# A fused attention and mixture-of-experts kernel: output scatters that do not wait for each other, early loads of the dense stage's first block, and a last block summed part by part

## Chip, cores and metric

One core of a Trainium2 chip runs the whole program. The metric is the time of one execution on the device, in microseconds (us); lower is better.

## What is computed

Three stages follow each other, all in float32 (B 4, H 8, S 576, D 64 in the attention; 2304 tokens of width 512 after it):

```python
q_rot, k_rot = rotate(q), rotate(k)                       # rotary embedding
attn = softmax(q_rot @ k_rot.T / sqrt(D)); x = attn @ v   # -> 2304 x 512
e = argmax(x @ w_gate); gate = softmax(x @ w_gate)[e]     # 8 experts, one per token
x = gate * (relu(x @ w1[e]) @ w2[e])                      # 512 -> 1024 -> 512
h = x @ moe2_w_in                                         # dense: 512 -> 2048 -> 512
out = (relu(h) ** 2) @ moe2_w_out
```

## The kernel before, in words

**Products.** TensorE multiplies in pairs: each operand is split into a high part (rounded by ScalarE) and a low part (what is left, subtracted on VectorE or GpSimd), and a product is three matmuls, high by high, high by low, low by high.

**Stages.** Attention takes 16 pairs of heads. The expert stage takes the tokens sorted by expert, in tiles of 128 rows: `Experts.run` (L916 to L922) loops over tiles `i` 2 to 17, and the last tiles sit in nested conditionals (`tail`, L941). The dense stage, `Dense.run` (L1096 to L1117), takes 6 blocks `b` of 384 rows; for each block 16 steps `f` compute 128 columns of h and add their share of the output.

**One step of the expert loop.** `begin(i)` is the first product of tile i into PSUM `p_h` (`first`, L861), the gather of tile i+2 (L843, an indirect transfer on POOL's queue), the transposes of tile i+1 (`turn_x`, L850), and `change(i+1, 0)` (L902): only if the expert changes, the first weight matrix W1 is split from its raw buffers (high parts on ScalarE L838, low parts L839, the second of the four chunks on POOL), and then the next expert's raw weights are loaded by SP (L817), each chunk once its buffer has been read. `second(i-1)` is the second product of the tile before (L890): VectorE scales it into `yo` (L894), and POOL scatters it to the DRAM buffer `yd` (L895). `end(i)` transposes tile i's relu (`turn_h`, L880) and does `change(i, 1)`, the same for W2 (loads L819). Then `extra(i - 2)` slips in work for the dense stage: its weights' loads and conversions (L962, L973 to L984) and, at the end of steps 14 to 16, `load_part` (L1037): one third of the dense stage's first block of 384 rows, read from `yd` by SP into `row`; one buffer holds all three in turn. At the end of steps 15 to 17, `turn_x(0, c)` (L1051 to L1053) transposes such a third into PSUM `p_r` and splits it. A third is thus loaded at the end of one step and transposed at the end of the next.

**Dependencies.** A tile framework places the waits, in the order in which the code names the instructions; it takes an indirect scatter to touch all of its target. Thus a `load_part` waits for the last scatter into `yd` named ahead of it, and the next scatter waits until that load has been read. Each engine and each DMA queue runs its own instructions in that same order, so one that waits holds up all behind it on its queue. SP issues all the plain loads here.

**The dense stage's end.** Two steps after `first(b, f)` (L1061), `second(b, f)` (L1074) adds the step's share to three PSUM tiles `o[c]`, one per 128 rows, three matmuls each (L1082). After step 15, `store` (L1085) copies them to SBUF `os` (ScalarE for c = 0 and 2, VectorE for c = 1) and POOL scatters each to `out` by the token ids in `id` (L1093):

```python
for f in range(16):          # lagging by two steps
    for c in range(3):       # o[c] += gs[f][c] @ Wo[f], three matmuls
```

Of the kernel before, what the change touches and what calls it, by code (L numbers as in the profile page):

```python
# [12 lines left out]
I32 = mybir.dt.int32  # L13
U32 = mybir.dt.uint32
AF = mybir.ActivationFunctionType
# [7 lines left out]
N, DM = B * S, H * D  # L23
# [3 lines left out]
NA = 2  # L27
# [32 lines left out]
def shape_constants():  # L60
# [27 lines left out]
    for b in range(B):  # L88
        for c in range(4):
# [22 lines left out]
           out=[33.418, 34.148, 36.917, 39.025, 37.411, 29.788, 32.958, 38.405, 36.294, 35.538, 34.643],  # L112
# [623 lines left out]
class Experts:  # L736
# [176 lines left out]
            self.load(m, e)  # L913
            self.split(m, ())

    def run(self, extra):  # L916
        for i in range(NA, 18):
            self.begin(i)
            self.second(i - 1)
            self.end(i)  # L920
            extra(i - NA)
        self.tail(18)  # L922
# [64 lines left out]
class Dense:  # L987


    def __init__(self, nc, ident, big, wip, words, wp, ps, y, out, w_in, w_out):  # L990
        self.nc, self.ident, self.big, self.words, self.wp, self.ps = nc, ident, big, words, wp, ps
        self.y, self.out, self.w_in, self.w_out = y, out, w_in, w_out
        self.wip = wip
        self.T = {}

    def load_in(self, j):
        self.T["wi", j] = self.words.load(self.w_in[:, 512 * j:512 * j + 512].rearrange("(k p) f -> p k f", p=128), 4)
# [73 lines left out]
        nc.scalar.activation(gs[:, 0], g, AF.Copy)  # L1071
        nc.vector.tensor_sub(gs[:, 1], g, gs[:, 0].bitcast(F32))  # L1072

    def second(self, b, f):  # L1074
        nc = self.nc
        if f == 0:
            self.T["o", b] = [self.ps.tile([128, 512], F32, name="o", tag=f"o{c}", bufs=1) for c in range(3)]
        gs, W = self.T["gs", b, f], self.T["Wo", f]
        for c in range(3):
            n = 0  # L1080
            for a, w in ((0, 0), (0, 1), (1, 0)):
                nc.tensor.matmul(self.T["o", b][c], gs[:, a, 128 * c:128 * c + 128], W[:, w], start=(f == 0 and n == 0), stop=(f == 15 and n == 2))  # L1082
                n += 1

    def store(self, b):  # L1085
        nc = self.nc
        for c in range(3):
            t = self.wp.tile([128, 512], F32, name="os", tag="os", bufs=3)
            if c == 1:
                nc.vector.tensor_copy(t, self.T["o", b][c])  # L1090
            else:
                nc.scalar.activation(t, self.T["o", b][c], AF.Copy)  # L1092
            nc.gpsimd.indirect_dma_start(out=self.out, out_offset=bass.IndirectOffsetOnAxis(ap=self.T["id", b][:, c:c + 1].bitcast(U32), axis=0),  # L1093
                                         in_=t, in_offset=None)

    def run(self):  # L1096
        nb, lag = N // 384, 2
        self.split_in(1)
        for i in range(16 * nb + lag):
            b, f = divmod(i, 16)  # L1100
            if b < nb:
                self.first(b, f)
                if i == 0:
                    self.split_out(0)
                if b == 0:
                    self.weights(f)
                if f == 2:
                    self.load_ids(b)
                    if b + 1 < nb:
                        self.load_x(b + 1)  # L1110
                if f in (10, 12, 14) and b + 1 < nb:
                    self.turn_x(b + 1, f // 2 - 5)
            if i >= lag:
                b2, f2 = divmod(i - lag, 16)
                self.second(b2, f2)
                if f2 == 15:
                    self.store(b2)  # L1117

    def weights(self, f):

# [14 lines left out]
def body(tc, a, cols):  # L1135
    nc = tc.nc
    stack = contextlib.ExitStack()
    with stack:
        pool = lambda name, bufs, **kw: stack.enter_context(tc.tile_pool(name=name, bufs=bufs, **kw))
        pp, dp = pool("p", 1), pool("d", 1, space=DRAM)  # L1140
        xd = dp.tile([N, DM], F32, name="xd")
        yd = dp.tile([N + 128, DM + 16], F32, name="yd")
        ident = pp.tile([128, 128], F32, name="ident")
        make_identity(nc, ident)
        tpool = lambda name, **kw: tc.tile_pool(name=name, bufs=1, reuse_waits="tile", **kw)
        rowp = contextlib.ExitStack()
        keep = stack.enter_context(tc.tile_pool(name="keep", bufs=1, side="right"))
        rows = rowp.enter_context(tc.tile_pool(name="row", bufs=1, side="right"))
        consts = rows.tile([128, a["consts"].shape[1]], F32, name="consts")
        cst = lambda n: consts[:, cols[n][0]:cols[n][1]]  # L1150
        R = Route(nc, pp, rows, keep, cst, ident)
        X = Experts(tc, R, rowp.enter_context(tc.tile_pool(name="raws", bufs=1, side="right")), ident, xd, yd, a["moe_w1"], a["moe_w2"])
        w1p = contextlib.ExitStack()
        with tc.manual_schedule():
            done, last = attention(tc, a["rope"], ident, a["qk"], a["v"], a["moe_w_gate"], xd, R.batch,
                                   lambda: nc.sync.dma_start(out=consts, in_=a["consts"]),
                                   lambda at, psum: X.ahead(at, psum, lambda n: w1p.enter_context(tpool(n, side="right"))))
            done.close()
            big, cvp, x0 = [stack.enter_context(tpool(n)) for n in ("big", "cv", "x0")]
            words = Words(nc, cvp)  # L1160
            dn = Dense(nc, ident, big, None, words, None, None, yd, a["out"], a["moe2_w_in"], a["moe2_w_out"])
            with w1p, tpool("xg") as xg, tpool("mw") as mw, tpool("mps", space=PSUM) as ps:
                X.late(big, xg, ps, mw)
                dn.xs0 = x0.tile([128, 2, 4, 384], F32R, name="xs0")
                spots = iter([X.p_r[:, 0:40].rearrange("p (c e) -> p c e", e=8), X.p_r[:, 64:72]])
                R.psum = lambda shape: next(spots)
                X.first(0, 0)
                X.first(0, 1)
                X.swap(0)
                X.relu(0)  # L1170
                next(last)
                next(last, None)
                R.places(dn.xs0)
                for n, eng in enumerate((nc.gpsimd, nc.vector)):
                    R.gated_rows(R.al[n], 10 * n, 10, eng)
                X.first(1)
                X.turn_h(0)
                X.relu(1)
                R.lists(X.p_r[:, 128:128 + 3 * NB].rearrange("p (i t) -> p i t", i=3))
                tokens = R.tokens()  # L1180
                next(tokens)
                X.gather(2)
                X.gather(3)
                R.control()
                next(tokens, None)
                X.second(0)
                X.turn_x(2)
                X.load(0, X.num(1, 0, mx=7, engines=(E.SP,)))
                X.change(2, 0)
                X.turn_h(1)  # L1190
                X.swap(1)
                X.load(1, X.num(1, 0, mx=7, engines=(E.SP,)))

                dn.y0 = R.row.rearrange("p c n -> p (c n)")[:, 2048:2560].bitcast(F32)
                dn.wi0 = R.row.rearrange("p c n -> p (c n)")[:, 0:2048].rearrange("p (a k f) -> p a k f", a=2, k=4)

                def extra(i):
                    if 13 <= i < 16:
                        dn.turn_x(0, i - 13, X.p_r.rearrange("p (k n) -> p k n", k=4))
                    if 12 <= i < 15:  # L1200
                        dn.load_part(i - 12)
                    if i == 14:
                        dn.split_in(0)
                    if i < 9:
                        if i < 8:
                            dn.load_in(i)
                        if i > 0:
                            dn.convert_in(i - 1)
                    if 10 <= i < 14:
                        dn.load_out(i - 10)  # L1210
                    if i in (11, 12):
                        dn.convert_out(i - 11)

                X.run(extra)
            rowp.close()
            with tpool("Wi", side="right") as wi, tpool("dw") as dw, tpool("dps", space=PSUM) as ps:
                dn.wip, dn.wp, dn.ps = wi, dw, ps
                dn.run()
# [25 lines left out]
```

## Time and profile before

| what | value |
|---|---|
| median of 3 runs (lowest to highest) | 992.5 us (991.63 to 993.58) |
| the profiled execution: its own time, and the span of its instructions | 993.26 us, 991.2 us |
| mean granted TensorE clock | 0.993 of full speed |
| TensorE matmuls busy | 955.0 us, 96% |
| VectorE, ScalarE, GpSimd busy | 534.3, 421.7, 320.3 us |
| stages by the timeline of TensorE | attention and routing, then expert tiles up to 573 us, then the dense blocks |

The span runs from the first instruction to the last; 2.06 us of the execution's own time lie around it. The share of busy time is a mean over stages with different limits, so what a change is worth has to be read from the stretch that it touches: who waits there, and what the wait is for.

### The profile page before, as it was taken

To read this page: it belongs to the slowest core of one execution; us is meant where nothing else is said; L and a number is where in the kernel's file an instruction comes from. 1 tells how busy PE (TensorE), PEld (TensorE's weight loads), DVE (VectorE), ACT (ScalarE), POOL (GpSimd) and SP (SyncE) were. 2 spreads that over 40 slices of the span, in tenths; PEclk is the share of its full clock that TensorE was granted. 3 is DMA by queue.
4 is the path that set the end of the run, shared out by engine and by line. 5 is a ranking of instruction groups with operands and counts; after the bars stand their busy time and mean duration, and the time that the engine had idled before them with its cause. 6 is when DMAs were issued, how large, how long until landed. Compare 5 with 4: busy or idle time off the path is not lost. (4 is left out here: it accounts for less than half of the span.)

```text
span 991.2 us, 15383 instructions
## 1 busy us (share of the span) xinstructions
PE 955.0 (96%) x5519; PEld 819.2 (83%) x5519; DVE 534.3 (54%) x935; ACT 421.7 (43%) x834; POOL 320.3 (32%) x241
## 2 busy tenths in 40 slices
PE   4999999999999999999979999999999999999995
PEld 4787878787778888888868789999999999999994
DVE  5677777777868255682884479423322223222221
ACT  3666666675542233442653367422322322222221
POOL 4786888796384111331453300010000100100101
PEclk9999999999999999999999999999999999999998
DMA  6776767775542733363575423100100100000000
GB/s 232 240 199 193 231 203 195 237 199 140 181 138 104 276 129 129 108 234 130 187 272 172 160 91 125 33 32 1 43 22 1 64 1 33 32 1 1 32 1 32
DMA packets 45135, 119.81 MB, mean 121 GB/s; under 512 B 8176, under 2 KB 8176, under 8 KB 42608
## 3 DMA queue, kind: packets, MB, share of 16 engines
q1 hardware_dynamic: 39808, 101.58, 32.8%
q0 software_dynamic: 4960, 16.43, 4.7%
q8 instruction: 45, 0.74, 0.3%
q10 hardware_dynamic: 272, 0.66, 0.2%
q14 instruction: 50, 0.41, 0.1%
HBM read 79.93 MB, written 15.11 MB: 96 GB/s over the span
## 5 line engine op out<-in xcount | busy, mean ns | idle before, releaser
L1082 PE MATMUL o<-Wo,gs 128*128 128x512 f32 x864 | 214.5, 393 | 0.0
L1061 PE MATMUL h<-xs,Wi 128*128 128x384 f32 x1008 | 189.6, 336 | 0.0
L1061 PEld LDWEIGHTS h<-xs,Wi 128*128 128x128 f32 x1008 | 178.1, 188 | 6.6
L1082 PEld LDWEIGHTS o<-Wo,gs 128*128 128x128 f32 x864 | 160.0, 188 | 28.3
L1070 DVE SCALAR_TENSOR_TENSOR g<-h,r 128x384 f32<-128x384 f32 x80 | 44.6, 558 | 190.7 <-ACT r L1066 190.7
L1093 POOL DMA_INDIRECT out_dram<-os,id x18 | 19.1, 1064 | 393.2 <-ACT os L1092 362.1
L293 ACT ACTIVATE e<-ps,mx 128x576 f32<-128x576 f32 x144 | 106.2, 740 | 84.8 <-DVE mx L286 84.7
L286 DVE TENSOR_REDUCE mx<-ps 128x1 f32<-128x576 f32 x144 | 105.9, 753 | 58.0 <-PE ps L278 50.5
L1066 ACT ACTIVATE r<-h 128x384 f32<-128x384 f32 x96 | 47.1, 491 | 204.6 <-PE h L1061 204.6
L890 PE MATMUL p_y<-W,hh 128*128 128x512 f32 x504 | 122.9, 399 | 0.8 <-ACTq L902 0.8
L861 PE MATMUL p_h<-W,xs 128*128 128x512 f32 x480 | 115.8, 397 | 0.0
L890 PEld LDWEIGHTS p_y<-W,hh 128*128 128x128 f32 x504 | 93.1, 188 | 22.2 <-ACTq L902 1.1
L861 PEld LDWEIGHTS p_h<-W,xs 128*128 128x128 f32 x480 | 89.2, 190 | 18.7 <-DVEq L902 0.7
L311 PE MATMUL pp<-ident,e 128*128 128x128 f32 x640 | 85.5, 273 | 2.1 <-DVE eT L327 1.9
L1072 DVE TENSOR_TENSOR gs<-g,gs 128x384 fp32r<-128x384 f32 x96 | 53.5, 558 | 55.9 <-ACT gs L1071 55.3
L433 POOL TENSOR_TENSOR qk<-qk,TB 128x1280 f32<-128x1280 f32 x28 | 81.4, 2924 | 0.0
L311 PEld LDWEIGHTS pp<-ident,e 128*128 128x128 f32 x640 | 74.4, 141 | 3.3 <-DVE eT L327 2.3
L276 PE MATMUL ps<-kZ,qZ 128*128 128x288 f32 x300 | 71.5, 328 | 0.5 <-ACT e L293 0.2
L1071 ACT ACTIVATE gs<-g 128x384 fp32r<-128x384 f32 x96 | 50.4, 525 | 50.4 <-DVE g L1070 49.9
L338 PE MATMUL av<-eT,V 128*64 128x288 f32 x512 | 69.1, 412 | 0.0
L327 DVE COPY eT<-pp 128x512 f32<-128x512 f32 x96 | 64.3, 684 | 4.6 <-PE pp L311 2.7
L895 POOL DMA_INDIRECT yd<-yo,idx x21 | 22.2, 1059 | 134.7 <-DVE yo L894 94.1
(236 smaller groups left out, 1210.4 us busy)
## 6 DMA issues: line engine op xcount, KB each, us to landing
qk<-in_qk_dram SPq DMA_DIRECT2D x15, 1280.0 KB, 6.4
raw<-in_moe_w_dram SPq DMA_DIRECT2D x30, 512.0 KB, 4.8
kZ<-XH SPq DMA_DIRECT2D x60, 160.0 KB, 2.8
rawa<-in_moe_w_dram SPq DMA_DIRECT2D x18, 512.0 KB, 3.5
w<-in_moe_w_in_dram SPq DMA_DIRECT2D x8, 1024.0 KB, 5.2
w<-in_moe_w_out_dram SPq DMA_DIRECT2D x8, 1024.0 KB, 4.9
V<-in_v_dram SPq DMA_DIRECT2D x16, 320.0 KB, 2.9
qZ<-XH SPq DMA_DIRECT2D x30, 160.0 KB, 2.9
```

What stands on the lines that cost most here:

```text
L276: nc.tensor.matmul(t[:, u, 0:288], Q1[:, qs], K1[:, k0 + 288 * u:k0 + 288 * u + 288], start=i == 0, stop=False)
L286: nc.vector.tensor_reduce(small("mx", P, 9)[:, s:s + 1], T["S", P, s][:, :, 0:288], axis=AX.XY, op=ALU.max, negate=True)
L293: nc.scalar.activation(ed.rearrange("p (u n) -> p u n", u=2), T["S", P, s][:, :, 0:288], AF.Exp, bias=T["mx", P][:, s:s + 1], accum_out=SS ...
L311: nc.tensor.transpose(t[:, c * 128:c * 128 + 128], src, ident)
L327: nc.vector.tensor_copy(o, i)
L338: nc.tensor.matmul(t[64 * j:64 * j + 64], V[:, j, kc], eT[:, j, kc, cs] if kc < 4 else eL[:, cs], start=kc == 0, stop=kc == 4)
L433: v.tensor_tensor(out=out, in0=a, in1=b, op=ALU.mult)
L861: nc.tensor.matmul(t[u], s[:, a, k], W1[:, b, k, 512 * u:512 * u + 512], start=n == 0, stop=n == 11)
L890: nc.tensor.matmul(t, s[:, a, k], W2[:, b, k], start=n == 0, stop=n == 23)
L1061: nc.tensor.matmul(t, W[:, a, k, fs], s[:, c, k], start=n == 0, stop=n == 11)
L1072: nc.vector.tensor_sub(gs[:, 1], g, gs[:, 0].bitcast(F32))
L1082: nc.tensor.matmul(self.T["o", b][c], gs[:, a, 128 * c:128 * c + 128], W[:, w], start=(f == 0 and n == 0), stop=(f == 15 and n == 2))
```

## The change

Three edits. `between(i - 2)`, a new hook, stands inside the step, behind `second(i-1)` and ahead of `end(i)`; the transposes and the loads of the dense block's thirds go from `extra` to it. `apart` declares the output scatters to be free of each other, and each scatter reads its ids from a small tile `at` that POOL copies first. For the last block the last two steps are done tile by tile: all that is left of `o[0]`, then its store, then `o[1]`, then `o[2]`; and each of these three stores is copied half by VectorE and half by ScalarE.

```diff
     def run(self, extra, between):
         for i in range(NA, 18):
             self.begin(i)
             self.second(i - 1)
+            between(i - NA)
             self.end(i)
             extra(i - NA)
...
+    def apart(self, ins):
+
+        self.tc.declare_no_dep(ins, group="out", reason="every token's row is written once")
+        self.tc.add_to_no_dep_group("out", ins)
...
+    def store(self, b, cs=range(3)):
...
-            if c == 1:
-                nc.vector.tensor_copy(t, self.T["o", b][c])
+            o = self.T["o", b][c]
+            if b == N // 384 - 1:
+                nc.vector.tensor_copy(t[:, 0:256], o[:, 0:256])
+                nc.scalar.activation(t[:, 256:512], o[:, 256:512], AF.Copy)
+            elif c == 1:
+                nc.vector.tensor_copy(t, o)
...
+            at = self.wp.tile([128, 1], I32, name="at", tag="at", bufs=3)
+            nc.gpsimd.tensor_copy(at, self.T["id", b][:, c:c + 1])
+            put = nc.gpsimd.indirect_dma_start(out=self.out, out_offset=bass.IndirectOffsetOnAxis(ap=at.bitcast(U32), axis=0),
+                                               in_=t, in_offset=None)
+            self.apart(put.ins)
...
-                self.second(b2, f2)
-                if f2 == 15:
-                    self.store(b2)
+                if b2 < nb - 1 or f2 < 16 - lag:
+                    self.second(b2, f2)
+                    if f2 == 15:
+                        self.store(b2)
+        for c in range(3):
+            for f in range(16 - lag, 16):
+                self.second(nb - 1, f, [c])
+            self.store(nb - 1, [c])
...
+                def between(i):
                     if 13 <= i < 16:
                         dn.turn_x(0, i - 13, X.p_r.rearrange("p (k n) -> p k n", k=4))
                     if 12 <= i < 15:
                         dn.load_part(i - 12)
+
+                def extra(i):
                     if i == 14:
                         dn.split_in(0)
```

SP's loads in step 15, before, from the last load of W1's raw weights on (`raw_3727`; `raw_3728` to `raw_3731` are W2's four raw chunks, `row<-yd` is the second third):

```order
L817 DMA raw_3727<-in_moe_w_dram 128x1024
...
L819 DMA raw_3728<-in_moe_w_dram 128x2x512
L819 ISA
L819 DMA raw_3729<-in_moe_w_dram 128x2x512
L819 ISA
L819 DMA raw_3730<-in_moe_w_dram 128x2x512
L819 ISA
L819 DMA raw_3731<-in_moe_w_dram 128x2x512
L902 UNCONDITIONAL_BRANCH x2
L1037 DMA row<-yd 128x512
L962 DMA w_6196<-in_moe_w_out_dram 128x2x1024
```

And now:

```order
L817 DMA raw_3727<-in_moe_w_dram 128x1024
L902 UNCONDITIONAL_BRANCH x2
L1043 DMA row<-yd 128x512
...
L819 DMA raw_3728<-in_moe_w_dram 128x2x512
L819 ISA
L819 DMA raw_3729<-in_moe_w_dram 128x2x512
L819 ISA
L819 DMA raw_3730<-in_moe_w_dram 128x2x512
L819 ISA
L819 DMA raw_3731<-in_moe_w_dram 128x2x512
L902 UNCONDITIONAL_BRANCH x2
L963 DMA w_6196<-in_moe_w_out_dram 128x2x1024
```

The load of the third has gone ahead of the four weight loads; steps 14 and 16 change alike. On TensorE, each of the three groups of four transposes `p_r` moves from behind the eight transposes `p_t` to ahead of them.

At the program's end, with what each instruction waits for (SW and HW are DMA queues' semaphores), ScalarE and POOL before, the last block's stores:

```order
L1092 ACTIVATE os<-o 128x512 [waits DMASW5_49,PE_49]
L1092 ACTIVATE os<-o 128x512 [waits DMASW7_49,PE_49]
...
L1093 DMA out_dram<-os,id 2304x512 [waits DMAHW0_49,DMASW7_49,Activation_49]
L1093 DMA out_dram<-os,id 2304x512 [waits DMASW0_49,DVE_49]
L1093 DMA out_dram<-os,id 2304x512 [waits DMASW1_49,Activation_49]
```

And now, the last two of the three (the first is alike):

```order
L1099 ACTIVATE os<-o 128x256 [waits DMASW3_49,DMASW6_49,DMASW0_49,DVE_49]
L1099 ACTIVATE os<-o 128x256 [waits DMASW7_49,DVE_49]
...
L1105 COPY at<-id 128x1 [waits DMASW6_49]
L1106 DMA out_dram<-os,at 2304x512 [waits Activation_49,Pool_49]
L1105 COPY at<-id 128x1 [waits DMASW7_49]
L1106 DMA out_dram<-os,at 2304x512 [waits Activation_49,Pool_49]
```

A scatter no longer waits for the DMA semaphore of the scatter ahead of it (the SW ones that are left on the copies are those of the block before, whose buffers they take over); POOL's copy of the ids stands between the scatters; and ScalarE's half of a store waits for VectorE, no longer for TensorE.

## Rows read from the trace of the kernel before

**Rows 1.** The page, section 1: busy time, share of the span, instructions.

```profile
PE 955.0 (96%) x5519; PEld 819.2 (83%) x5519; DVE 534.3 (54%) x935; ACT 421.7 (43%) x834; POOL 320.3 (32%) x241
```

**Rows 2.** Waits of TensorE, 455 to 577 us: who for whom, us, times, longest.

```profile
PE p_r L1051 <- DMA row<-yd: 5.6, 1, 5.6
```

**Rows 3.** Timeline of TensorE: start, us, line, out<-in, count, idle before it.

```profile
488.86 5.85 PE L890 MATMUL p_y<-W,hh 128*128 128x512 f32 x24
...
501.69 5.85 PE L890 MATMUL p_y<-W,hh 128*128 128x512 f32 x24
...
507.38 1.03 PE L880 MATMUL p_t<-ident,hs 128*128 128x128 f32 x8
513.98 1.09 PE L1051 MATMUL p_r<-ident,row 128*128 128x128 f32 x4 [5.56 <-DMA row<-yd]
514.72 6.67 PE L861 MATMUL p_h<-W,xs 128*128 128x512 f32 x24
...
521.57 5.84 PE L890 MATMUL p_y<-W,hh 128*128 128x512 f32 x24
...
528.48 5.72 PE L861 MATMUL p_h<-W,xs 128*128 128x512 f32 x24
```

**Rows 4.** Windows: us, busy us (instructions) by engine, TensorE clock, DMA share, GB/s.

```profile
514.00:516.00 2.00, 2.00 (x7) 1.81 (x8) 1.58 (x3) 1.42 (x3) 1.35 (x1) 0.50 0.48 146
```

**Rows 5.** Timeline of SP's queue in steps 15 and 16.

```profile
501.21 4.84 SPq L819 DMA_DIRECT2D raw<-in_moe_w_dram  x4
506.42 0.34 SPq L1037 DMA_DIRECT2D row<-yd  x1
```

**Rows 6.** By tile or line: issue to landing of `row`, W2 raw weights, `yd` scatters.

```profile
DMA to landing us min/median/max: 2.6/6.1/7.4
...
DMA to landing us min/median/max: 4.4/5.9/7.4
...
DMA to landing us min/median/max: 2.8/2.9/7.3
```

**Rows 7.** Timelines of VectorE, GpSimd and ScalarE in steps 15 and 16.

```profile
498.12 0.74 DVE L894 TENSOR_SCALAR yo<-p_y,sg 128x512 f32<-128x512 f32 x1
...
499.64 1.01 POOL L895 DMA_INDIRECT yd<-yo,idx  x1 [2.53 <-issue]
...
514.65 2.00 POOL L895 DMA_INDIRECT yd<-yo,idx  x1 [8.94 <-DVE W L839]
...
513.46 1.06 ACT L838 ACTIVATE W<-raw 128x1024 fp32r<-128x1024 f32 x1 [0.58 <-SPq L902]
```

**Rows 8.** Timeline of the end of the span, all engines.

```profile
978.36 0.60 ACT L1092 ACTIVATE os<-o 128x512 f32<-128x512 f32 x1 [3.11 <-PE o L1082]
...
979.23 0.97 POOL L1093 DMA_INDIRECT out_dram<-os,id  x1 [52.80 <-ACT os L1092]
979.74 0.60 ACT L1092 ACTIVATE os<-o 128x512 f32<-128x512 f32 x1 [0.78 <-PE o L1082]
982.75 0.97 POOL L1093 DMA_INDIRECT out_dram<-os,id  x1 [2.54 <-DMA out_dram<-os,id]
986.58 0.97 POOL L1093 DMA_INDIRECT out_dram<-os,id  x1 [2.86 <-issue]
```

**Rows 9.** Landing of the output scatters; two gathers in a row; a small copy.

```profile
DMA to landing us min/median/max: 2.7/2.7/3.1
...
272.29 1.21 POOL L843 DMA_INDIRECT xg<-xd,idx  x1 [6.80 <-DVE sg L656]
273.80 0.96 POOL L843 DMA_INDIRECT xg<-xd,idx  x1 [0.30 <-issue]
...
569.48 0.20 POOL L893 COPY yo<-idx 128x16 int32<-128x16 int32 x1 [1.84 <-DMA yd<-yo,idx]
```

**Rows 10.** Groups by form: line, engine, op, shapes, count | us, mean ns.

```profile
L367 DVE TENSOR_TENSOR xr<-pj,rs 128x256 f32<-128x256 f32 x16 | 6.6, 415 | 0.0
...
L341 ACT ACTIVATE X<-av 128x288 f32<-128x288 f32 x32 | 12.8, 409 | 7.4 <-PE av L338 7.4
```

More of the change, by code (lines that the diff above doesn't have):

```diff
@@ L914, in swap, with run @@
             self.split(m, ())
-    def run(self, extra):
+    def run(self, extra, between):
         for i in range(NA, 18):
@@ L987, with __init__ @@
 class Dense:
-    def __init__(self, nc, ident, big, wip, words, wp, ps, y, out, w_in, w_out):
-        self.nc, self.ident, self.big, self.words, self.wp, self.ps = nc, ident, big, words, wp, ps
+    def __init__(self, tc, ident, big, wip, words, wp, ps, y, out, w_in, w_out):
+        self.tc, self.nc, self.ident, self.big, self.words, self.wp, self.ps = tc, tc.nc, ident, big, words, wp, ps
         self.y, self.out, self.w_in, self.w_out = y, out, w_in, w_out
@@ L1072, in first, with second @@
         nc.vector.tensor_sub(gs[:, 1], g, gs[:, 0].bitcast(F32))
-    def second(self, b, f):
+    def second(self, b, f, cs=range(3)):
         nc = self.nc
@@ L1078, in second @@
         gs, W = self.T["gs", b, f], self.T["Wo", f]
-        for c in range(3):
+        for c in cs:
             n = 0
@@ L1083, in second @@
                 n += 1
-    def store(self, b):
+    def store(self, b, cs=range(3)):
         nc = self.nc
-        for c in range(3):
+        for c in cs:
             t = self.wp.tile([128, 512], F32, name="os", tag="os", bufs=3)
-            if c == 1:
-                nc.vector.tensor_copy(t, self.T["o", b][c])
-            else:
-                nc.scalar.activation(t, self.T["o", b][c], AF.Copy)
-            nc.gpsimd.indirect_dma_start(out=self.out, out_offset=bass.IndirectOffsetOnAxis(ap=self.T["id", b][:, c:c + 1].bitcast(U32), axis=0),
-                                         in_=t, in_offset=None)
+            o = self.T["o", b][c]
[4 more added lines that the diff above has]
+                nc.vector.tensor_copy(t, o)
+            else:
+                nc.scalar.activation(t, o, AF.Copy)
+            at = self.wp.tile([128, 1], I32, name="at", tag="at", bufs=3)
[3 more added lines that the diff above has]
+            self.apart(put.ins)
     def run(self):
@@ L1160, in body @@
             words = Words(nc, cvp)
-            dn = Dense(nc, ident, big, None, words, None, None, yd, a["out"], a["moe2_w_in"], a["moe2_w_out"])
+            dn = Dense(tc, ident, big, None, words, None, None, yd, a["out"], a["moe2_w_in"], a["moe2_w_out"])
             with w1p, tpool("xg") as xg, tpool("mw") as mw, tpool("mps", space=PSUM) as ps:
@@ L1195, in body @@
                 dn.wi0 = R.row.rearrange("p c n -> p (c n)")[:, 0:2048].rearrange("p (a k f) -> p a k f", a=2, k=4)
-                def extra(i):
+                def between(i):
                     if 13 <= i < 16:
@@ L1212, in extra @@
                         dn.convert_out(i - 11)
-                X.run(extra)
+                X.run(extra, between)
             rowp.close()
```

## The prediction

> **What bounds the kernel now.** I read the page first: TensorE is busy for 96% of the span [rows 1]. So time can be won where TensorE idles or runs slowly, and where the program goes on after its last matmul, and lost by new idle time on it. The waits of TensorE in the late expert tiles then name one long one: 5.6 us, once, for the transfer into `row` [rows 2]. TensorE's timeline shows its place: the transposes `p_r` of the second third, at 513.98 us [rows 3].
>
> What the wait costs is more than its length, and the same rows give it. From one `second` to the next is 501.69 - 488.86 = 12.83 us in step 15, whose transposes waited for nothing. In step 16 it is 521.57 - 501.69 = 19.88 us. The excess is 7.05 us: 5.56 of idle time, and the rest from slow matmuls behind it. The first product took 6.67 us where it takes 5.72 [rows 3], at a granted clock of 0.50 [rows 4], the lower of the two levels (1.2 of 2.4 GHz), after the idle time.
>
> Why was the third late? Its load stands on SP's queue behind four loads of W2's raw weights; these go out from 501.21 us on, as their buffers come free, and the third's goes out at 506.42 [rows 5]. It takes the full 7.4 us to land, as long as the slowest weight load in front of it [rows 6]. A second victim is POOL's scatter into `yd`, which had to wait until 514.65 [rows 7] for that load to be done with `yd`.
>
> Last, the end. The last matmul ends near 979.7 us, when the third copy starts; then three scatters follow each other 3.5 and 3.8 us apart, at 979.23, 982.75 and 986.58 [rows 8], each waiting for the one before, which takes 2.7 us to land [rows 9]. From the start of the last one to the end of the span are 991.2 - 986.58 = 4.62 us, which stay: landing, and the program's closing.
>
> **The change, part one: the thirds.** Nothing is added; three loads and three sets of transposes move.
>
> The second third's load now stands ahead of the four weight loads. What it waits for next is the scatter of the tile before, named just ahead of it: that goes out at 499.64 us and takes a median 2.9 us to land [rows 6, 7], so the load goes out at 502.55, 3.9 us earlier than before. With no weight load in front of it I take the shortest landing of such a load, 2.6 us [rows 6]: 505.2 us. TensorE wants it behind `second`, at 507.38 [rows 3]. The wait goes, with 2.2 us to spare: 7.05 us.
>
> The first third waited for nothing before; its load now goes out behind a scatter too, a few us ahead of its transposes. The third third goes out only after SP has passed the next conditional, which is held until the last W2 load has landed (before, that was near 513.4 us, just ahead of ScalarE's split at 513.46 [rows 7]). Say 515; with the median 6.1 us [rows 6] it lands at 521, while TensorE would be at it one step later than 507.38, at 507.38 + 12.83 = 520.2. With 2.6 us it lands at 517.6. The bounds are thus 0 and about 0.9 us; I take 0, since only the 1 MB load of dense weights may lie in front of it.
>
> What is late next: W2's weights. They are queued behind a load that waits. The first of them goes out at 503.0, not 501.21; the other three are held by their buffers until about 503.5 to 505.8, as before. In front of them are 0.25 MB more. The 2 MB took from 501.21 to 513.46, so an eighth more is 1.5 us, and the last lands near 515 us rather than 513.4. Its high part needs 1.06 us on ScalarE [rows 7]: ready at 516.1. TensorE, no longer held, starts that `second` at 501.69 + 12.83 = 514.52 and reads the last chunk of W2 at its seventh matmul, 6 x 0.24 us later (24 take 5.84 [rows 3]), at 515.96. I book 0.3 us of new waiting (bounds 0 and 1.1, if the loads slip by 0.8 more). ScalarE and VectorE take the third's split 0.6 to 0.7 us earlier in the step, ahead of the relu's split; VectorE's loss falls within the time in which its second subtraction of W2 was blocked, so the buffers come free as before. If that cover is missing, it is in the 1.1 us. POOL's scatter moves from 514.65 to about 509.1; it is off the path.
>
> Part one: 7.05 - 0.3 = **6.75 us**, between 5.0 and 7.05.
>
> **Part two: the end.** TensorE does the same matmuls, so it ends as before. But the first sum is done after 15 of the last 27 matmuls, not after 21. Two sums are 979.74 - 978.36 = 1.38 us apart [rows 8], six matmuls, so the first is ready at 978.36 - 1.38 = 976.98, the second at 978.36, the third, as ever, at 979.74.
>
> Each copy is cut in two, but the order of the instructions shows ScalarE's half waiting for VectorE's, so they add up. VectorE's nearest row of that size is 0.415 us (reading PSUM), ScalarE's 0.409 for 288 columns [rows 10]; I take 0.39 for 256 and 0.03 between. That is 0.84 us, against 0.60 for a whole copy [rows 8]: the cut costs 0.24 us. Were the halves to run side by side it would gain 0.18 us. No row has two engines reading one PSUM tile. The Trainium skill, PSUM — Partial Sum Buffer, section "PSUM bank collisions raise a hardware error", says that two engines must not touch the same bank and partitions at once, reads included; by that rule the halves can only add up, and no run here shows it.
>
> From VectorE's `yo` to its scatter POOL took 499.64 - 498.86 = 0.78 us [rows 7]; ScalarE's copy to the scatter of [rows 8] took 0.27, with nothing but that wait left. Now a semaphore instruction stands in front again, so I take 0.78. The first scatter starts at 976.98 + 0.84 + 0.78 = 978.60 and holds POOL for 0.97. Then come the small copy of ids, 0.20, and a scatter that waits for nothing more, 0.30 behind it as between two gathers [rows 9]: 1.47 us from scatter to scatter. The second starts at 980.07, the third at 981.54; its own copy would allow 979.74 + 0.84 + 0.78 = 981.36. Two transfers in flight are nothing new: two gathers went out 1.5 us apart [rows 9], less than any landing of an indirect transfer in these rows. The end is then 981.54 + 4.62 = 986.16: **5.04 us** saved.
>
> Bounds: POOL free and a lag of 0.27 give 980.85 + 4.62, 5.7 us (6.2 if the halves also overlap). The longest lag is that of the last scatter, 986.58 - (982.75 + 2.73) = 1.1 us; paid three times, the third starts at 983.4: 3.2 us.
>
> The 15 earlier scatters and their copies of ids lie beside TensorE's work, which nothing there waits for; without that cover each copy would be 0.20 us.
>
> **Sum.** 6.75 + 5.04 = 11.8 us off the profiled execution's 993.26: 981.5 us. That execution lies 0.8 above the median of 992.5, so I forecast **980.7 us**.
>
> **Rivals.**
> - *The third is still late.* If the load at 502.55 takes 7.4 us all the same, because weights issued behind it share the engines, it lands at 509.95: TensorE waits 2.6 us, with a like share of slow matmuls (1.49 x 2.57 / 5.56 = 0.7). Part one shrinks to 3.8 us: 983.7 us. For it: landings vary from 2.6 to 7.4. Against: the 7.4 had loads in front. 12%.
> - *The scatters stay slow*, with the long lag each: 3.2 us in place of 5.0, 982.5 us. For it: the lag did vary from 0.27 to 1.1. 14%.
> - *The scatters are not free of each other after all*, or share something that the order doesn't show: the first starts at 978.60 rather than 979.23, and the rest follow as before; 0.6 us saved, 985.1 us. Against: the DMA semaphores are gone from the waits. 2%.
> - *Slower: weights in place of the third.* SP stands before the third's load until the scatter lands, and W2's weights stand behind it. The longest such landing was 7.3 us [rows 6]: load at 506.9, weights from 507.3, the last some 12 us later at 519.6, its high part at 520.7, so TensorE waits 4.7 us, and part one is down to about 1. To eat part two and 2 us more, the weights have to be 14 us late, landing after 529 us: 995 us. That is the point from which it decides; that 7.3 itself waited among weight loads. 2%.
> - *The halves run side by side* or POOL is quicker: 979.6 us. 3%.
>
> **How the numbers follow.** The forecast's own case has the remaining 67%, from 979.4 (7.05 and 5.7 us) to 982.3. Range: low is the best of both, 7.05 and 6.2 us, less the 0.9 us by which the fastest run shown lies under the median: 978.4. High takes in the late third and the slow scatters each by itself: 984.0; both together and the rest are left out. A measurement of this kernel tells about 0.2%, 2 us, from no change; all but the last rival's 2% and a remainder of 1% lie beyond that on the fast side.
>
> **What would show it.** In the waits of TensorE no wait for `row`, and the spacing of `second` near 12.8 us in step 16, with at most a fraction of a us for the split of W2; SP's third ahead of the four weight loads at about 502.5. At the end, three scatters about 1.5 us apart, the first near 978.6 less what was won before, ScalarE's halves starting when VectorE's end, 4.6 us from the last scatter's start to the end. Wrong would be a new wait of TensorE for W2 of over 1.1 us, a landing of the second third of over 5 us, or scatters still 3.5 us apart.

## The result, and the profile after

The changed kernel takes 981.35 us (median of 4 runs, 980.48 to 983.31), the kernel before beside it 992.41 us (4 runs): a ratio of 0.989, 95% interval 0.9871 to 0.9909. The forecast was 980.7 us. Measured once more, with other runs of the kernel before (992.39), it took 981.36 us, ratio 0.9886 (0.987 to 0.9901). The profiled execution took 982.04 us with a span of 980.2 us, 11.0 us less than the 991.2 us of the one before. One execution of e2 below took 1365.34 us at a mean granted clock of 0.656 and stays out of its numbers.

The page after, section 1, answers to [rows 1]: TensorE is busy 1.2 us less, and its mean granted clock is 0.997, against 0.993.

```profile
PE 953.8 (97%) x5519; PEld 818.1 (83%) x5519; DVE 531.9 (54%) x937; ACT 421.5 (43%) x835; POOL 322.5 (33%) x259
```

Waits of TensorE after, 455 to 577 us (who for whom, us, times, longest), to be held against [rows 2]:

```profile
PE p_r L1057 <- DMA row<-yd: 1.2, 1, 1.2
...
PE p_y L890 <- ACT W L838: 0.6, 1, 0.6
```

The wait for `row` is down from 5.6 to 1.2 us, not to nothing, and one for W2's split has come. Their place, in TensorE's timeline after (start, us, line, out<-in, count, idle before), beside [rows 3]:

```profile
487.62 5.85 PE L890 MATMUL p_y<-W,hh 128*128 128x512 f32 x24
...
500.45 5.85 PE L890 MATMUL p_y<-W,hh 128*128 128x512 f32 x24
507.47 0.66 PE L1057 MATMUL p_r<-ident,row 128*128 128x128 f32 x4 [1.16 <-DMA row<-yd]
...
514.69 1.65 PE L890 MATMUL p_y<-W,hh 128*128 128x512 f32 x6
516.92 4.47 PE L890 MATMUL p_y<-W,hh 128*128 128x512 f32 x18 [0.58 <-ACT W L838]
...
522.46 5.74 PE L861 MATMUL p_h<-W,xs 128*128 128x512 f32 x24
```

I measure part one from the first row to the last: 522.46 - 487.62 = 34.84 us, against 528.48 - 488.86 = 39.62 us in [rows 3]: **4.78 us** won, where 6.75 were forecast. It splits by step. Step 15 to 16 takes 514.69 - 500.45 = 14.24 us, 1.41 over the 12.83 of a step without a wait; from that `second` to the next first product are 7.77 us, where 6.92 are needed without a wait (experiment e10 below), 0.85 over. And 7.05 - 1.41 - 0.85 = 4.79.

SP's queue after (start, us, line) shows why; it answers to [rows 5]:

```profile
503.68 0.33 SPq L1043 DMA_DIRECT2D row<-yd  x1
505.51 2.33 SPq L819 DMA_DIRECT2D raw<-in_moe_w_dram  x4
```

The third does go out ahead of the four weight loads, but at 503.68, 5.3 us after the scatter at 498.39 for which it waits, and the weights another 1.83 us later.

The end after, all engines, beside [rows 8]:

```profile
971.04 0.42 DVE L1098 COPY os<-o 128x256 f32<-128x256 f32 x1 [1.15 <-PE o L1088]
971.50 0.38 ACT L1099 ACTIVATE os<-o 128x256 f32<-128x256 f32 x1 [2.20 <-DVE os L1098]
...
972.66 0.98 POOL L1106 DMA_INDIRECT out_dram<-os,at  x1 [55.88 <-ACT os L1099]
...
973.65 0.19 POOL L1105 COPY at<-id 128x1 int32<-128x1 int32 x1
973.79 0.42 DVE L1098 COPY os<-o 128x256 f32<-128x256 f32 x1 [0.95 <-PE o L1088]
974.12 0.98 POOL L1106 DMA_INDIRECT out_dram<-os,at  x1 [0.28 <-POOL at L1105]
...
975.58 0.99 POOL L1106 DMA_INDIRECT out_dram<-os,at  x1 [0.28 <-POOL at L1105]
```

Three scatters 1.46 us apart. From the start of the third sum's copy to the end are 980.2 - 973.79 = 6.41 us, against 991.2 - 979.74 = 11.46 us before: **5.05 us** won, 5.04 forecast. The rest of the 11.0 us, 1.2, was there before the moved instructions began: the `second` of step 14 starts at 487.62 against 488.86. Of that, 1.1 us arose near 267 us, where TensorE waited twice in the execution before, 0.23 us and then:

```profile
267.57 1.22 PE L311 MATMUL pp<-ident,e 128*128 128x128 f32 x8 [0.85 <-DVE eT L327]
```

### The profile page after: what moved, and what is told of

It reads as the page before. It is cut to its first block, busy times and chain, and to the rows that moved or that the text cites. A ratio compares the mean times of both kernels' runs of the same rounds, so it can differ in the third digit from the quotient of the medians.

```text
span 980.2 us, 15407 instructions
## 1 busy us (share of the span) xinstructions
PE 953.8 (97%) x5519; PEld 818.1 (83%) x5519; DVE 531.9 (54%) x937; ACT 421.5 (43%) x835; POOL 322.5 (33%) x259
## 5 line engine op out<-in xcount | busy, mean ns | idle before, releaser
L1106 POOL DMA_INDIRECT out_dram<-os,at x18 | 17.8, 986 | 369.5 <-DVE os L1101 309.9
L895 POOL DMA_INDIRECT yd<-yo,idx x21 | 21.2, 1012 | 124.8 <-DVE yo L894 90.4
```

## Experiments

In the list below "stretch" is the time from the `second` of step 14 to the first product of step 17 (39.62 us before, 34.84 after), and "end" that from the start of the third sum's copy to the end of the span (11.46 and 6.41).

**The parts alone.** e1 is the change without its end:

```diff
-                if b2 < nb - 1 or f2 < 16 - lag:
-                    self.second(b2, f2)
...
-            if b == N // 384 - 1:
-                nc.vector.tensor_copy(t[:, 0:256], o[:, 0:256])
...
-            self.apart(put.ins)
```

> Only the first part of the change: loads and transposes of the thirds in the middle of the step, the end as it was. If the changed trace is read rightly, this part is worth 6.00 us of TensorE's time between step 14 and the first dense products, of which 1.24 us were there before the moved instructions began. Theory (those 1.24 us are chance): about 4.8 us off the kernel before, 987.6 us against 992.4. Rival A (they come with the change, for instance because moved code lies elsewhere): about 6.0 us off, 986.4 us. Rival B (the forecast's 6.75 us hold and the changed profile was taken in an odd execution): 985.7 us. In the trace the theory expects a wait of TensorE for the second third near 1.2 us and one for W2's split near 0.6 us.

Measured: 986.39 us, ratio 0.9946 (0.9933 to 0.9959) to 992.38 us: 6.0 us off by the medians, and the interval, 4.1 to 6.6 us, doesn't tell the theory from the rivals. The trace does, and not for rival A: the stretch itself is 33.79 us, 5.83 less. There is no wait for `row` here; W2's is 0.65 us. So the 1.2 us in the profile of the change came by chance, by which of the two executions waited near 267 us (e8 below, with the changed code, waits near 267 us as the kernel before did; e2, with the old thirds, doesn't), and it also lost more than e1 at the moved place. My expectation of 4.8 us had taken one late landing for the rule.

e2 is the change without its thirds:

```diff
-                def between(i):
+                def extra(i):
                     if 13 <= i < 16:
                         dn.turn_x(0, i - 13, X.p_r.rearrange("p (k n) -> p k n", k=4))
```

> Only the second part: free output scatters, the last block part by part with halved copies; the thirds as they were. Theory: 5.05 us off the kernel before, 987.4 us against 992.4, three last scatters 1.46 us apart, and TensorE's wait for the third back at 5 to 6 us. Rival (part of this gain came from the thirds, because the scatters or the weights before the end ran differently): less than 4 us off. If the 1.24 us that the changed profile was ahead by step 14 also show up here, 6.3 us off.

Measured: 987.04 us, ratio 0.9952 (0.9939 to 0.9965): 5.3 us off by the medians. End 985.3 - 978.90 = 6.40 us; the wait for `row` is 5.2 us again. The parts add up: 6.0 + 5.3 = 11.3 against 11.0 to 11.1 for both.

**The end taken apart.** e5 keeps only the free scatters, e6 only the order of the sums and the halves; e4 is the change with whole copies. The edit of e4:

```diff
-            if b == N // 384 - 1:
-                nc.vector.tensor_copy(t[:, 0:256], o[:, 0:256])
-                nc.scalar.activation(t[:, 256:512], o[:, 256:512], AF.Copy)
-            elif c == 1:
+            if c == 1:
```

> The changed kernel without the halving: the last block's sums are copied whole, by ScalarE, VectorE, ScalarE, as in the other blocks. Theory (the halves add up, and the three scatters' pitch of 1.46 us on GpSimd sets the end, so only the first copy counts): each copy 0.60 instead of 0.84 us, all three scatters start 0.2 us earlier after the first sum, 0.2 us off the changed kernel, 981.1 us, too little for the clock but to be seen in the trace. Rival A (the halves do win time, because two engines share the work): 0.2 us slower, 981.6 us. Rival B (a scatter that waits for VectorE rather than ScalarE has another lag): the middle pitch differs from 1.46 us.

> Of the second part only the freed scatters, with the small copies of the ids; the last block's steps in the order of before, whole copies, and the thirds as they were. Theory: the first scatter starts 0.3 us later than before at most (its copy of ids stands ahead), the others 1.46 us behind each other: from the third copy's start (ScalarE) to the end of the span 0.78 less 0.6 and 0.3 of lag, then 2.9 and 4.62, about 7.2 us against 11.46 before and 6.41 with all of part two; 4.2 us off the kernel before, 988.2 us. So freeing the scatters is worth some 4.2 of 5.05 us, and summing part by part 0.8 us. Rival (the reordering matters more, since the first sum is ready 1.4 us earlier): less than 3.7 us off.

> Of the second part only the last block's sums part by part with halved copies; the scatters still wait for each other, and the thirds are as they were. Theory (the chain of scatters sets the end, only its first link moves): the first scatter starts some 0.5 us earlier against the last matmul than before, the others 3.5 and 3.8 us behind each other; 0.6 us off, 991.8 us, not to be told from no change by the clock. With 3.95 us for the freed scatters alone (e5) and 5.05 for both, the order of the sums is worth 0.6 us before the scatters are free and 1.1 after. Rival (the two add up independently): 1.1 us off.

The third copies and the last scatters, from the timelines of e4, then e5, then e6:

```profile
972.23 0.60 ACT L1100 ACTIVATE os<-o 128x512 f32<-128x512 f32 x1 [2.15 <-PE o L1088]
973.78 0.99 POOL L1103 DMA_INDIRECT out_dram<-os,at  x1 [0.28 <-POOL at L1102]
```

```profile
978.69 0.60 ACT L1099 ACTIVATE os<-o 128x512 f32<-128x512 f32 x1 [0.78 <-PE o L1087]
981.61 0.98 POOL L1102 DMA_INDIRECT out_dram<-os,at  x1 [0.28 <-POOL at L1101]
```

```profile
977.75 0.97 POOL L1103 DMA_INDIRECT out_dram<-os,id  x1 [51.67 <-ACT os L1098]
...
979.38 0.42 DVE L1097 COPY os<-o 128x256 f32<-128x256 f32 x1 [0.95 <-PE o L1087]
...
981.26 0.97 POOL L1103 DMA_INDIRECT out_dram<-os,id  x1 [2.55 <-DMA out_dram<-os,id]
985.09 0.97 POOL L1103 DMA_INDIRECT out_dram<-os,id  x1 [2.86 <-issue]
```

e4: end 978.3 - 972.23 = 6.07 us, 0.34 better than with the halves: they do add up, and the cut costs time, as the forecast had it (0.24; the end is 6.07 to 6.12 us in the three profiles with whole copies, e4, e9 and e10, and 6.39 to 6.48 in the six with halves). By the clock 980.25 us (980.11 to 980.57), ratio 0.988 (0.9866 to 0.9894); of its 1.1 us against the change, which the intervals don't tell from nothing, the end explains a third; the stretch, 33.37 us, is shorter too, but whole copies don't touch it: that is the spread of part one (below). e5: end 986.2 - 978.69 = 7.51 us, 3.95 off, and 988.43 us by the clock, ratio 0.9958 (0.9945 to 0.9971), also 3.96 off. e6: end 989.7 - 979.38 = 10.32 us, 1.14 off; 992.19 us against 992.89, ratio 0.9991 (0.9982 to 1.0), by the clock not to be told from nothing. So freeing is worth 3.95 us and the reordering 1.14, and they add up (5.09 against 5.05): here the rival was right. My 0.6 us had charged the first scatter a lag of 0.78 us; in e6, where the scatters have no copy `at` and still wait for each other, it is 977.75 - 977.47 = 0.28. Which of the two makes the difference no run shows.

**Where part one lost 2 us.** e3 was meant to have each load named ahead of the scatter that it waits for:

```diff
+            between(i - NA)
             self.second(i - 1)
-            between(i - NA)
             self.end(i)
```

> The changed kernel with the new hook one place further up: the thirds' transposes and loads stand ahead of second(i-1), not behind it. SP's order is the same, but each load is now named ahead of the scatter of this step, so it waits only for the scatter of the step before and for the transposes that free its buffer; it lands a whole step before it is wanted. Theory (the missing 2 us of part one went to SP standing at the third's load until the scatter just sent off has landed, and to the loads of W2 behind it): no wait of TensorE for row, W2's first load out near 502.8 us instead of 505.5, at most 0.3 us of waiting for W2's split; 2.0 to 2.3 us off the changed kernel, 979.1 to 979.4 us. Rival A (W2's weights are late because another 0.25 MB stands in front of them and shares the engines): the wait for row goes, that for W2 stays; 1.4 us off, 980.0 us. Rival B (the two waits cost nothing, other things set the pace): 981.4 us.

Measured: 988.24 us, ratio 0.9961 (0.9949 to 0.9974): 7 us slower than the change, against every theory. TensorE waits for `row` three times. Its second third, on SP's queue and on TensorE:

```profile
498.46 0.33 SPq L1043 DMA_DIRECT2D row<-yd  x1
501.35 0.39 SPq L819 DMA_DIRECT2D raw<-in_moe_w_dram  x1
```

```profile
504.49 0.63 PE L1057 MATMUL p_r<-ident,row 128*128 128x128 f32 x4 [2.28 <-DMA row<-yd]
...
520.85 1.09 PE L1057 MATMUL p_r<-ident,row 128*128 128x128 f32 x4 [3.35 <-DMA row<-yd]
521.59 6.80 PE L890 MATMUL p_y<-W,hh 128*128 128x512 f32 x24
```

I had overlooked what stands ahead of the load on SP's own queue: W1's loads, held by their buffers until 498 us. Against the `second` of step 14 (489.60 here) the load goes out 8.9 us later, in the change 16.1 us: 7 us earlier, not a whole step. It lands 6.0 us after it went out, not 2.7, and is wanted ahead of a `second`, 6 us earlier than in the change. The scatter that is now named behind the load waits for it, up to 8.5 us. The load's wait for the scatter is gone here, so this run tells nothing on its price. The next one does: tiles from 11 on write no row of `yd` below 384 (tile 11 begins at row 1408 less at most 127 for each of seven changes of expert, 519), so a load of these rows needs to wait only for older scatters, with no instruction moved.

```diff
+        if i >= 11:
+            self.tc.declare_no_dep(put.ins, group="yd", reason="tiles from 11 on write no row below 384")
+            self.tc.add_to_no_dep_group("yd", put.ins)
```

(The thirds' loads join the same group.) e9 is this with whole copies, as e4.

> The changed kernel as it is, run beside the next two. Theory: the second third's load leaves when the scatter in front of it has landed, some 5 us after that went out (4.7 to 5.3 in the profiles so far, not the 2.9 of the forecast), so it lands within 0.4 us of the moment TensorE wants it, on either side; executions without a wait for row are near 980.5 us, those with one up to 2 or 3 us longer, median 980.5 to 981.5 us. Rival (the spread has another cause): the profile differs from its earlier one in other places than this step.

> The changed kernel with one wait less: the thirds' loads no longer wait for the scatters of tiles from 11 on, which write no row below 384. Order and place of all instructions stay. Theory: the second third's load goes out right behind W1's last raw load, near 497.5 us instead of 503, so TensorE never waits for row; SP reaches W2's loads some 2 us behind it and is then held by their buffers alone, first of them out near 500 to 501 us instead of 505, and the wait for W2's split (0.5 to 0.65 us) goes too. 0.6 us off an undisturbed execution and 1.0 to 1.5 us off the changed kernel's median: 979.8 us, with a narrower spread. Rival A (bandwidth: the third, in front of W2's 2 MB, makes them late wherever it goes out): the wait for W2 stays near 0.5 us, 980.4 us. Rival B (the third is now in flight beside W1's last loads, lands after 6 to 7 us and holds those up): TensorE waits for W1's split in front of the next first product, 981 us or more.

> The one before, with the last block's sums copied whole as in e4. Theory: 0.2 to 0.35 us less than that one (e4's end, from the third copy's start to the end of the span, was 6.07 us against 6.41), 979.5 us, the fastest of all. Rival: no difference from the one before, so that e4's 1.1 us came from the thirds' step alone.

Measured in one comparison: the change 981.36 us (980.29 to 981.65), e8 980.54 us (979.64 to 981.53), ratio 0.9878 (0.9862 to 0.9895), e9 979.03 us (978.56 to 979.30), ratio 0.9864 (0.9849 to 0.9879). TensorE in the change, then in e8:

```profile
487.83 5.85 PE L890 MATMUL p_y<-W,hh 128*128 128x512 f32 x24
...
516.32 4.46 PE L890 MATMUL p_y<-W,hh 128*128 128x512 f32 x18 [1.03 <-ACT W L838]
...
521.85 5.72 PE L861 MATMUL p_h<-W,xs 128*128 128x512 f32 x24
```

```profile
488.66 5.85 PE L890 MATMUL p_y<-W,hh 128*128 128x512 f32 x24
...
516.17 4.47 PE L890 MATMUL p_y<-W,hh 128*128 128x512 f32 x18 [0.19 <-ACT W L838]
...
521.70 5.72 PE L861 MATMUL p_h<-W,xs 128*128 128x512 f32 x24
```

The stretch is 34.02 us in the change, now with no wait for `row` but 1.03 us for W2, and 33.04 and 32.97 us in e8 and e9. The four profiles with the change's thirds (the change twice, e1, e4) have 33.37 to 34.84 us, 34.0 in the mean, so by the traces **1.0 us** was the wait for the scatter; the first profile lost more, by its own late third (1.41 us in that step). The clock doesn't tell e8 from the change. Nor does e9's lead of 1.5 us on e8 come from the copies: the ends differ by 0.27 us and the stretches by 0.07, while e8's profile was 1.87 us behind by the `second` of step 14, with the wait near 267 us in it. Rival B's long landing came, 5.2 and 6.3 us for the third, but no wait for W1. And W2's loads did not come as early as expected. SP's queue in e8:

```profile
498.65 0.33 SPq L1046 DMA_DIRECT2D row<-yd  x1
504.01 1.04 SPq L819 DMA_DIRECT2D raw<-in_moe_w_dram  x2
```

That is 504.01 - 488.66 = 15.35 us behind the `second` of step 14, where it was 501.21 - 488.86 = 12.35 before and 17.89 after. SP was free; the buffer was not. What frees it is VectorE's first subtraction of W2 (in e8 it ends at 503.98), and in the change it is slow. VectorE and GpSimd in the second execution of the change:

```profile
499.54 3.60 DVE L839 TENSOR_TENSOR W<-raw,W 128x1024 fp32r<-128x1024 f32 x1
```

```profile
499.64 2.41 POOL L839 TENSOR_TENSOR W<-raw,W 128x1024 fp32r<-128x1024 f32 x1
```

Both start together, and VectorE takes 3.6 us. e10 is e9 with VectorE's low part of the third behind W2's conditional; e11 does only that to the change.

```diff
                 def extra(i):
+                    if 13 <= i < 16:
+                        dn.turn_low(i - 13, X.p_r.rearrange("p (k n) -> p k n", k=4))
```

> e9 (loads free of the late scatters, whole copies) with one more move: VectorE's subtraction for the third's low part goes back behind the step's conditional for W2; transposes and ScalarE's high part stay. In the profiles so far VectorE's first subtraction of W2 takes 3.6 us where the third's low part stands ahead of it, because it then starts together with GpSimd's subtraction of its own chunk (2.4 us), and 1.2 us before the change, where it was done just before GpSimd began. Theory (that moved start is what holds W2's first load, 15.3 us after the second of step 14 in e9 and e8 against 12.35 before): the first subtraction takes 1.2 us again, the second 3.4, and W2's first load goes out 12.4 us after the second of step 14; the second product of step 16 takes 5.85 us instead of 6.24, so 0.4 us off e9, 978.6 us. Rival (VectorE is slow there for another reason, e.g. ScalarE's split beside it): still 3.4 to 3.6 us for the first.

> The changed kernel with only that move of VectorE's subtraction; the loads still wait for the scatter just sent off. Theory (two things hold W2's loads in series, the buffer and SP's wait, and SP's is the later): the buffer is free 3 us earlier, but W2's first load still goes out some 17.5 us after the second of step 14, and the time stays at the changed kernel's 981.4 us within 0.4. Rival (the blocked subtraction alone is the loss, the scatter's wait costs nothing): W2's first load near 15 us or less behind the second of step 14, no wait for W2's split, 980.5 us.

VectorE, then SP, then TensorE in e10:

```profile
498.47 1.21 DVE L839 TENSOR_TENSOR W<-raw,W 128x1024 fp32r<-128x1024 f32 x1
```

```profile
499.71 0.39 SPq L819 DMA_DIRECT2D raw<-in_moe_w_dram  x1
```

```profile
487.37 5.85 PE L890 MATMUL p_y<-W,hh 128*128 128x512 f32 x24
...
500.20 5.85 PE L890 MATMUL p_y<-W,hh 128*128 128x512 f32 x24
505.89 0.60 PE L1062 MATMUL p_r<-ident,row 128*128 128x128 f32 x4
...
513.04 5.85 PE L890 MATMUL p_y<-W,hh 128*128 128x512 f32 x24
...
519.96 5.74 PE L861 MATMUL p_h<-W,xs 128*128 128x512 f32 x24
```

The subtraction takes 1.21 us, W2's first load goes out 499.71 - 487.37 = 12.34 us behind the `second`, TensorE waits for nothing in the stretch, and it is 519.96 - 487.37 = 32.59 us, 7.03 under the kernel before. By the clock e10 is 979.48 us beside 992.89, ratio 0.9861 (0.9846 to 0.9876), the same as e9; 0.4 us are too little to be seen there. e11: 982.04 us, ratio 0.9889 (0.9874 to 0.9904), a stretch of 34.75 us, W2's first load 17.73 us behind the `second`: no gain, as the theory had it, since SP stands at the scatter anyway. It was even 0.6 us over the 981.4, with a wait of 1.49 us for W2; why that wait is longer than the 1.03 of the change stays open.

## Why the prediction held, point by point

**The bound.** That the 5.6 us wait in the late tiles costs 7.05 us with its slow matmuls is shown by e10, which takes all of it away: 7.03 us against the profile before. The price isn't fixed: in e2, e5 and e6, with the thirds as before, the wait was 5.2 to 5.9 us, the slow product behind it took 6.69 to 8.00 us, and the stretch 39.95 to 41.25 us.

**Part one, the load's time: the step that failed.** "that goes out at 499.64 us and takes a median 2.9 us to land [rows 6, 7], so the load goes out at 502.55". The order was right, the size was not. The scatter has W1's last loads beside it, and from its start to that of the third's load are 5.29, 4.85, 5.03, 4.74 and 5.14 us in the five profiles of this code (the change twice, e1, e4, and e11 with one subtraction moved). The median was taken over scatters that mostly had the DMA engines to themselves: 13 of the 21 landed in 2.8 to 3.1 us, with the engines busy for 0.23 to 0.27 of that time. The trace before had the landing of this very scatter (`L895`, 496 to 502 us), with the engines busy for 0.89 of it:

```profile
DMA to landing us min/median/max: 4.2/4.2/4.2
```

With that row the forecast's own sum has the load out at 503.84 and 0.9 us to spare, not 2.2. In the event none was left: the third was in time, to within 0.2 us, four times of five, and 1.16 us late once, for 1.41 us in all. The late third among the rivals was to cost 3 us.

**Part one, W2.** I booked 0.3 us, between 0 and 1.1. It cost 0.85 and 1.43 us in the two profiles of the change, 1.16 and 0.78 in e1 and e4. Two steps were off. "the buffers come free as before" was wrong: the third's low part, 0.67 us on VectorE, pushes its first subtraction onto GpSimd's, and the blocked one is then the first, not the second. And between the third's load and W2's first one I had 0.45 us; it was 1.83, the reads of the conditional's control values included, since SP makes them only behind the load. The buffer freed early gives nothing by itself (e11), the scatter's wait lifted by itself some 1.0 us (e8, e9), and both together the 7.03 us (e10).

**Part one in sum.** 4.78 us in one profile, below my lower bound of 5.0, and 5.60 in the other; e1's clock says 6.0. The bound was too tight because it let W2 (1.1 us) and the third third (0.9) vary, but not the second third. The first profile was also an unlucky pair: over the four with the thirds as before (the kernel before, e2, e5, e6) the stretch has a mean of 40.2 us, over the four with the change's 34.0, so part one is worth 6.2 us in the mean.

**Part two.** 5.05 us against 5.04. First scatter 0.78 us after its copy (0.78 forecast), pitch 1.46 (1.47), 4.62 from the last start to the end (4.62). The halves: 0.42 + 0.38, and ScalarE's starts as VectorE's ends. That they don't overlap is the program's order, so the rule of the Trainium skill, PSUM — Partial Sum Buffer, section "PSUM bank collisions raise a hardware error", was not put to the test.

**The rivals.** The free scatters are free (e5). The long lag did not come, nor weights 14 us late. The late third came in part, and not as told: its load went out late, behind the scatter. In the one profile in which TensorE had to wait, it could start 3.79 us after the load's issue; in the change's other profile, e1 and e4 the load landed in 2.7 us.

**The sum.** 4.78 + 5.05 + 1.2 = 11.0 us in the profiled pair; 6.0 + 5.3 by the clocks of the parts. The 1.2 us in the pair is luck: without it the pair would have missed the forecast by 2 us, all of it in part one. With the mean stretches it is 6.2 + 5.05 = 11.25 us. The forecast took 11.8 us off and the medians show 11.1: the missing 0.7 us goes with part one, whose mean is 0.6 us short of the 6.75.

## What to carry to other kernels

A load that is moved ahead in a queue takes its waits along: before the move, ask for the time between the thing waited for and its release in that very stretch, with the traffic there, and not for a median over the program; then ask what stands behind it on the queue. Where the wait is only the framework's caution (rows that never meet), declaring the two free of each other gives back part of what the move alone leaves, 1.0 us here. And of two engines that subtract at the same time, look at which one starts first: a move of 0.7 us can turn the order round and hold a buffer for 3 us.

## What the runs showed of the hardware

- VectorE's subtraction of a 128x1024 chunk takes 1.21 us alone and 3.60 us when GpSimd's of the same kind (2.41 us) starts within 0.1 us of it: 1.21 + 2.41 = 3.62, as if it had stood still for all of it. The Trainium skill, SBUF — State Buffer, section "Who interferes with whom", says that such pairs exclude each other and the later one blocks. The sum agrees; by the starts shown VectorE was 0.10 us ahead, and lost all the same. In e10, with VectorE 0.7 us ahead, GpSimd took 2.77 us.
- A scatter of 128 rows into `yd` released its waiter after 4.7 to 5.3 us beside W1's last weight loads; over the kernel before the median was 2.9 us [rows 6]. There, 13 scatters landed in 2.8 to 3.1 us with the DMA engines busy for at most 0.27 of that time, one in 2.8 us at 0.52, and seven in 4.0 to 7.3 us at 0.62 to 0.99. The time goes with the traffic; that W1's loads are the cause in step 15 no run shows, since none takes them away.
- TensorE's clock after short waits: in e3, idle for 2.28 us, the next product took 5.84 us at a granted clock of 1.00; idle for 3.35 us, it took 6.80 us, and the granted clock was 0.50, the lower of the two levels, from 520.85 to 521.6 us, 0.58 from 522 to 524, and 1.00 from 524 to 528. After the change's 1.16 us it stayed at 1.00 (508 to 512 us). My price for a late third had slow matmuls for any wait.
- A scatter that waits for ScalarE alone started 0.28 us after the copy (e6); in the kernels with GpSimd's small copy `at` and freed scatters, 0.77 to 0.78 us (the change, e4, e5).
